# Choosing the early expert with the eight-largest instruction, and loading and converting the second expert's first layer before the first job

## The chip, the cores and the metric

The kernel runs on one core of one Trainium2 chip. The metric is device time in microseconds (us) of one execution; lower is better. Times of before: 698.91 us median of 3 runs (697.92 to 702.77).

## The reference

Three layers follow one another on 3072 tokens of 320 values.

```
attention:  an m-LSTM over 4 x 8 heads of 768 steps, head size 40 (gates f, i, o; state C, n, m)
x = attn_out, as 3072 rows of 320
MoE 1:      logits = x @ w_gate; e = argmax(logits)          # one of 8 experts for each token
            gate_w = softmax(logits)[e];  eom = sigmoid(x @ w_output_gate)
            out[e's tokens] = gate_w * eom * (relu(x @ w1[e]) @ w2[e])     # 320 -> 1024 -> 320
MoE 2:      (sigmoid(x @ w_gate) * (x @ w_val)) @ w_out                    # 320 -> 1536 -> 320
```

## The kernel before

**Stages.** Attention runs in 24 chunks of 128 tokens (`step(n)`, with the order of parts in the tables `ORDER` and `LAST`). While a chunk is in work, the tokens of earlier chunks get their logits (`log`, `lg_`), are routed (`route`, a generator of which the parts named `r:2` and `r:3` take two or three pieces) and are scattered by GpSimd (POOL) into `xs_d` in memory, where each expert has its own stretch of rows. Then come the jobs of MoE 1, one for each expert, from that with the most rows down, and then MoE 2 in 8 groups of 384 tokens.

**The early expert.** After 16 chunks (`EARLY`), `first_expert` picks the expert with the most rows so far. Its number, its first row and its end are put into `first_i`; SyncE (SP) loads them into registers (`first_weights`, L924; `first_end`, L259) and starts loading this expert's weights (`load_weights`, at steps 20, 21 and 22). 256 rows of this expert (`HEAD`) are computed in `Head` while the last chunks are still being routed. `sort_experts` ranks the others when routing ends.

**The jobs.** `Job.up(w1, f)` makes eight slices `f` of the hidden layer: 8 matmuls each, then ScalarE (ACT) writes the high half of relu (L362) and VectorE (DVE) the low half (L363). `Job.down(w2, i)` multiplies 128 rows by the second layer, hidden slice after hidden slice (`k` = 0 to 7, three matmuls each, L373). The first job (`jobs[0]`) holds the remaining 256 of the early expert's 512 slots, so its downs come to 48 matmuls.

**The weights.** An expert's weights arrive as fp32 in a staging tile `ws` (pool `stage`, four buffers) and are split into a high and a low fp16 half by ACT (L118) and DVE (L119), in pieces of at most 512 columns. One expert is six units: units 0 to 2 are the first layer `w1`, two pieces each; units 3 to 5 are `w2`. `Feed` holds the units in order: `load` issues loads up to three units ahead, `pull(budget)` puts in as many pieces as a budget allows (it is called in each `up` and `down`), and `drain(upto)` puts in all pieces up to a unit. `load_next` issues the first loads for the second expert in the tail of attention; `there=step.next` tells the feed so.

**Blank rows.** `blanks(k)` writes filler rows behind an expert's last row in `xs_d`, so that its job can read a full slot; the job's transposing read of `xs_d` (L352) and its small read `own` (L353) come behind them. All of these and the loads of weights are issued from SP's one queue, in its order.

**What sets the order.** Each engine runs its instructions in a fixed order made at build time. The builder places an instruction on its engine by when it expects it to be ready, so the order of calls in the code is not always that of the rows; the rows of the section on the change show what came out.

Of the kernel before, what the change touches and what calls it, by code (L numbers as in the profile page):

```python
# [9 lines left out]
F32 = mybir.dt.float32  # L10
F16 = mybir.dt.float16
U32 = mybir.dt.uint32
I32 = mybir.dt.int32
# [8 lines left out]
T = 128  # L22
# [44 lines left out]
def fused(ctx, tc, a, out, dbg=None):  # L67
# [30 lines left out]
    def constants():  # L98
        G.memset(fill, 0.0)
        G.tensor_copy(fill[:, XW - 2:XW - 1].bitcast(U32), tok[:, NTILE:])  # L100
        split(wgl[:, 0], wgl[:, 1], wgl_s, SG)
        G.tensor_copy(rows_e, ebase)
        G.tensor_copy(table[:, 0], num_e)
        G.tensor_copy(table[:, 1], ebase[0:1])
# [128 lines left out]
    first_e = perm.tile([1, E], F32, name="first_e")  # L233
    first_i = perm.tile([1, 3], I32, name="first_i")
    table = perm.tile([1, 3, E], F32, name="table")
    plan = perm.tile([1, 3, E], U32, name="plan")
    rank = perm.tile([1, 2, E], F32, name="rank")

    def by_tokens(key):

        V.tensor_sub(key, rows_e[0:1], ebase[0:1])
        V.scalar_tensor_tensor(key, key, float(E), last_e, ALU.mult, ALU.add)

    def first_expert():
        f2 = small.tile([1, 4], F32, name="f2", bufs=1)
        by = small.tile([1, 3, E], F32, name="planf", bufs=1)
        G.tensor_copy(table[:, 2], rows_e[0:1])
        by_tokens(key)
        V.tensor_reduce(f2[:, 3:4], key, AX.X, ALU.max)
        yield  # L250
        V.tensor_tensor(first_e, key, f2[:, 3:4].to_broadcast([1, E]), ALU.is_equal)
        V.tensor_tensor(by, table, first_e.unsqueeze(1).to_broadcast([1, 3, E]), ALU.mult)
        V.tensor_reduce(f2[:, 0:3], by, AX.X, ALU.add)
        V.tensor_copy(first_i, f2[:, 0:3])
        yield

    def first_end():

        return nc.sync.value_load(first_i[0:1, 2:3], min_val=0, max_val=(E - 1) * PITCH + EARLY * T)  # L259

    key = perm.tile([1, E], F32, name="key")

    def sort_experts():

        top = small.tile([1, E], F32, name="top", bufs=1)
        by_tokens(key)
        V.scalar_tensor_tensor(key, first_e, 2.0**20, key, ALU.mult, ALU.add)
        V.max(top, key)
        V.max_index(plan[:, 0], top, key)
        V.tensor_scalar_mul(plan[:, 1], plan[:, 0], float(PITCH))  # L270
# [129 lines left out]
    with ExitStack() as att:  # L400
# [521 lines left out]
        def first_weights():  # L922

            e, step.row = (nc.sync.value_load(first_i[0:1, i:i + 1], min_val=0, max_val=(E - 1) * m)  # L924
                           for i, m in enumerate((1, PITCH)))
            return of_expert(e)
# [20 lines left out]
        def load_next():  # L947

            w1, _ = of_expert(place(ranks[1])[0])
            for k in range(3):  # L950
                s = stage.tile([128, F1], F32, name="ws", tag="ws")
                if k == 0:
                    G.memset(s[0:1, 0:8], 0.0)
                SP_.dma_start(out=s, in_=w1[:, k])
                step.next.append(s)
# [320 lines left out]
    with ExitStack() as m1:  # L1276
# [20 lines left out]
        for k, (r, s, n) in enumerate(jobs):  # L1297
            ahead += 0.95 * idle[k]
            if k + 1 < E:
                r1 = ranks[k + 1]  # L1300
                weights[r1] = expert_tiles(wfA if (k + 1) % 2 == 0 else wfB)
                feed.add(expert_units(*weights[r1], lambda r=r1: of_expert(place(r)[0]), there=(None,) * 3 if k else step.next))
# [11 lines left out]
        with tc.manual_schedule(engines=manual):  # L1314
# [17 lines left out]
            at_work = {0: job(0)}  # L1332
            blanks(1)
            feed.load()
            for k, (r, s, n) in enumerate(jobs):
# [4 lines left out]
                rate = feed.left(upto[k]) / idle[k]  # L1340
                w1, w2 = weights[r]
                for f in range(K1):
                    if f == K1 // 2 and k + 2 < len(jobs):
                        blanks(k + 2)
                    cur.up(w1, f, lambda: feed.pull(rate * idle_up(n, f), upto[k]))
# [80 lines left out]
def _constants():  # L1426
# [23 lines left out]
    ctab[..., 2 * TMAX + 1] = E - 1 - np.arange(E)  # L1450
# [41 lines left out]
```

## Time and profile before

| | |
|---|---|
| median of 3 runs | 698.91 us |
| the profiled execution | 699.65 us |
| its span, from the first to the last instruction | 697.9 us |
| TensorE (PE) busy | 669.2 us (96%) |
| VectorE (DVE) busy | 395.0 us (57%) |
| ScalarE (ACT) busy | 301.7 us (43%) |
| GpSimd (POOL) busy | 121.3 us (17%) |
| mean granted TensorE clock | 0.988 |

The profile is of one execution. Busy times overlap, since the engines run side by side; an engine's idle time costs something only where another that sets the end waits for it. The timeline gives the start of each group of instructions from the span's start, how long it took, and in brackets how long the engine was idle just before it and what released it. The stages that matter here lie at 105 to 117 us (the early expert is chosen) and at 138 to 172 us (end of attention, the first job, start of the second job).

### The profile page before, as it was taken

The numbers are of one execution on the slowest core, as the hardware profiler recorded it, in microseconds if no ns is written. First come the engines' busy times: TensorE is split into PE (matmuls) and PEld (weight loads), VectorE is DVE, ScalarE is ACT, GpSimd is POOL, SyncE is SP. The second block draws the span as 40 slices with busy tenths as digits, with TensorE's granted clock in tenths as the row PEclk, the third lists the DMA queues.
The fourth block names the chain that finished last, engine by engine and source line by source line (L and its number), as shares of the span: only waits on it lengthen the run. The fifth ranks groups of instructions, "written<-read, shape, count | busy, mean of one in ns | idle before, by whom it ended". The sixth has DMA issues, their size and how long they took to land. (4 is left out here: it accounts for less than half of the span.)

```text
span 697.9 us, 16215 instructions
## 1 busy us (share of the span) xinstructions
PE 669.2 (96%) x6464; PEld 451.6 (65%) x6464; DVE 395.0 (57%) x930; ACT 301.7 (43%) x710; POOL 121.3 (17%) x192
## 2 busy tenths in 40 slices
PE   7898998798999999999989999999999999999998
PEld 4787887675666757667545576565665655656655
DVE  6688788767778788997858901322404214033131
ACT  2486776564566564654525511222313223133131
POOL 5335766341112222222100000000000000000000
PEclk9999999999999999999999999999999999999999
DMA  6567886569598998966333022001020010000000
GB/s 194 163 191 214 248 238 223 176 194 288 169 271 245 269 284 253 257 170 138 124 92 92 1 72 54 1 20 44 1 63 0 20 44 1 29 1 11 20 1 28
DMA packets 69727, 85.57 MB, mean 123 GB/s; under 512 B 44329, under 2 KB 51914, under 8 KB 69650
## 3 DMA queue, kind: packets, MB, share of 16 engines
q1 hardware_dynamic: 66160, 75.05, 38.8%
q0 software_dynamic: 2896, 9.22, 3.7%
q8 instruction: 51, 0.84, 0.5%
q10 hardware_dynamic: 594, 0.25, 0.2%
q14 instruction: 26, 0.21, 0.1%
HBM read 57.36 MB, written 18.04 MB: 108 GB/s over the span
## 5 line engine op out<-in xcount | busy, mean ns | idle before, releaser
L132 PE MATMUL pa<-xT,wgv 128*128 128x384 f16 x1348 | 226.4, 328 | 3.7 <-DVEq L1369 3.2
L132 PEld LDWEIGHTS <-wgv 128*128 128x128 f16 x1348 | 130.3, 98 | 96.7 <-issue 13.9
L1251 DVE SCALAR_TENSOR_TENSOR gt<-pa,sg 128x384 f32<-128x384 f32 x96 | 52.9, 557 | 219.2 <-ACT sg L1250 204.0
L1269 PE MATMUL pb<-wo,hh 128*128 128x320 f16 x864 | 118.7, 299 | 0.1
L1250 ACT ACTIVATE sg<-pa 128x384 f32<-128x384 f32 x96 | 45.9, 485 | 142.2 <-PE pa L1239 142.0
L1269 PEld LDWEIGHTS <-hh 128*128 128x128 f16 x864 | 84.0, 98 | 34.8 <-issue 2.6
L373 PE MATMUL pb<-w,hh 128*128 128x320 f16 (+4 forms) x624 | 88.3, 303 | 3.0 <-ACT hh L362 2.7
L132 PEld LDWEIGHTS <-w 128*128 128x128 f16 x704 | 61.4, 98 | 31.8 <-issue 0.6
L132 PE MATMUL pa<-xT,w 128*128 128x384 f16 (+5 forms) x576 | 80.8, 301 | 0.0
L373 PEld LDWEIGHTS <-hh 128*128 128x128 f16 (+4 forms) x624 | 63.4, 102 | 26.6 <-ACT hh L362 3.1
L119 DVE SCALAR_TENSOR_TENSOR w<-ws,w 128x512 f16<-128x512 f32 (+1 forms) x92 | 56.6, 642 | 3.3 <-ACT w L118 3.3
L118 ACT ACTIVATE w<-ws 128x512 f16<-128x512 f32 (+1 forms) x92 | 51.2, 591 | 12.3 <-DMA ws<-in_w 12.3
L1255 ACT ACTIVATE hh<-gt 128x384 f16<-128x384 f32 x96 | 49.9, 520 | 10.8 <-DVE gt L1251 10.6
L1256 DVE TENSOR_TENSOR hh<-gt,hh 128x384 f16<-128x384 f32 x96 | 52.8, 550 | 1.6
L1271 ACT ACTIVATE ob<-pb 128x320 f32<-128x320 f32 x24 | 10.5, 437 | 85.1 <-PE pb L1269 85.1
L384 POOL DMA_INDIRECT y_d<-yr,own x24 | 28.8, 1200 | 77.4 <-DVE w L119 24.6
L363 DVE SCALAR_TENSOR_TENSOR hh<-pa,hh 128x384 f16<-128x384 f32 (+6 forms) x80 | 36.2, 479 | 10.7 <-ACT hh L362 10.2
L690 DVE TENSOR_TENSOR pf<-ps,w 128x512 f32<-128x512 f32 x48 | 31.2, 684 | 17.3 <-ACT w L675 6.5
L362 ACT ACTIVATE hh<-pa 128x384 f16<-128x384 f32 (+6 forms) x80 | 33.2, 431 | 13.8 <-PE pa L132 13.2
L720 PE MATMUL po<-vk,pf 128*64 128x41 f32 x768 | 28.7, 234 | 5.8 <-DVE po L709 3.5
L720 PEld LDWEIGHTS po<-vk,pf 128*64 128x64 f32 x768 | 25.9, 141 | 8.1 <-DVE po L709 4.3
L685 PE MATMUL ps<-qk 64*64 64x128 f32 x768 | 29.0, 287 | 1.8 <-issue 0.9
(188 smaller groups left out, 671.5 us busy)
## 6 DMA issues: line engine op xcount, KB each, us to landing
ws<-in_w SPq DMA_DIRECT2D x24, 512.0 KB
vk<-in_vk SPq DMA_DIRECT2D x24, 484.0 KB
qk<-in_qk SPq DMA_DIRECT2D x48, 160.0 KB
ws<-in_w SPq DMA_DIRECT2D x15, 480.0 KB
ws<-in_wg SPq DMA_DIRECT2D x9, 512.0 KB
ws<-in_wv SPq DMA_DIRECT2D x9, 512.0 KB
ws<-in_wo SPq DMA_DIRECT2D x8, 480.0 KB
out<-ob SPq DMA_DIRECT2D x24, 160.0 KB
```

The source lines that it names most:

```text
L118: A.activation(hi, src, AF.Copy, scale=scale)
L119: low = lambda: V.scalar_tensor_tensor(lo, src, scale, hi, ALU.mult, ALU.subtract)
L132: PE.matmul(ps, r if swap else l, l if swap else r, start=fresh and n == 0, stop=whole and n == len(steps) - 1, skip_group_check=not fresh)
L362: A.activation(self.hh[:, 0, f], ph, AF.Relu)
L363: V.scalar_tensor_tensor(self.hh[:, 1, f], ph, 0.0, self.hh[:, 0, f], ALU.max, ALU.subtract)
L373: PE.matmul(py, self.hh[:, x, k, sl], w2[:, y, k, :], start=k == 0 and x + y == 0, stop=k == K1 - 1 and x == 1)
L720: PE.matmul(m.po[sl, h, :], m.pf[g][:, p, sl], m.v41[:, h, :], start=m.first and h == 0, stop=g == 1, skip_group_check=True)
L1250: A.activation(sg, pgv[0], AF.Sigmoid, scale=1.0 / (SY * SWG))
L1251: V.scalar_tensor_tensor(gt, pgv[1], SGT / (SY * SWV), sg, ALU.mult, ALU.mult)
L1255: A.activation(self.gh[:, 0, f, :], box[0], AF.Copy)
L1256: V.tensor_sub(self.gh[:, 1, f, :], box[0], self.gh[:, 0, f, :])
L1269: PE.matmul(po, self.gh[:, x, k, sl], wo[:, y, k * DM:(k + 1) * DM], start=k == 0 and x + y == 0, stop=k == K2 - 1 and x == 1)
```

## The change

The parts:

1. `first_expert` finds the expert by one multiply-add (`by_tokens`; the constant `last_e` in `ctab` now takes the row base off too), `max` and `max_index` (`by_rank`), a multiplication (`starts`) and a copy of the row ends, in three pieces instead of two. The `table` on POOL, its three copies, the comparison, product and sum are gone. `first` holds all eight experts in rank order; `first_end` reads its end at the place given by a register.
2. `load_next` loads two units instead of three; the third comes from the feed.
3. Right after the first job's reads are issued, `feed.load()` and `feed.drain(3)` load units 2 to 5 and convert units 0 to 2, and only then `blanks(1)` follows. The first three slices of the first job pull nothing.

```diff
@@ constants
-        G.tensor_copy(table[:, 0], num_e)
-        G.tensor_copy(table[:, 1], ebase[0:1])
@@
-    def by_tokens(key):
-        V.tensor_sub(key, rows_e[0:1], ebase[0:1])
-        V.scalar_tensor_tensor(key, key, float(E), last_e, ALU.mult, ALU.add)
+    def by_tokens():
+        V.scalar_tensor_tensor(key, rows_e[0:1], float(E), last_e, ALU.mult, ALU.add)
+
+    def by_rank(to):
+        V.max(top, key)
+        V.max_index(to[:, 0], top, key)
+
+    def starts(to):
+        V.tensor_scalar_mul(to[:, 1], to[:, 0], float(PITCH))
 
     def first_expert():
-        f2 = small.tile([1, 4], F32, name="f2", bufs=1)
-        by = small.tile([1, 3, E], F32, name="planf", bufs=1)
-        G.tensor_copy(table[:, 2], rows_e[0:1])
-        by_tokens(key)
-        V.tensor_reduce(f2[:, 3:4], key, AX.X, ALU.max)
+        by_tokens()
         yield
-        V.tensor_tensor(first_e, key, f2[:, 3:4].to_broadcast([1, E]), ALU.is_equal)
-        V.tensor_tensor(by, table, first_e.unsqueeze(1).to_broadcast([1, 3, E]), ALU.mult)
-        V.tensor_reduce(f2[:, 0:3], by, AX.X, ALU.add)
-        V.tensor_copy(first_i, f2[:, 0:3])
+        by_rank(first)
         yield
+        starts(first)
+        V.tensor_copy(first[:, 2], rows_e[0:1])
+        yield
@@ sort_experts
-        by_tokens(key)
+        V.tensor_tensor(first_e, key, top[:, 0:1].to_broadcast([1, E]), ALU.is_equal)
+        by_tokens()
         V.scalar_tensor_tensor(key, first_e, 2.0**20, key, ALU.mult, ALU.add)
-        V.max(top, key)
-        V.max_index(plan[:, 0], top, key)
-        V.tensor_scalar_mul(plan[:, 1], plan[:, 0], float(PITCH))
+        by_rank(plan)
+        starts(plan)
@@ load_next
-            for k in range(3):
+            for k in range(2):
@@ the feed's list of units
-                feed.add(expert_units(..., there=(None,) * 3 if k else step.next))
+                feed.add(expert_units(..., there=(None,) * 3 if k else (*step.next, None)))
@@ ahead of the jobs
             at_work = {0: job(0)}
+            feed.load()
+            feed.drain(3)
             blanks(1)
-            feed.load()
             for k, (r, s, n) in enumerate(jobs):
...
-                rate = feed.left(upto[k]) / idle[k]
+                skip = 0 if k else 3
+                rate = feed.left(upto[k]) / (idle[k] - skip * idle_up(n, 0))
...
-                    cur.up(w1, f, lambda: feed.pull(rate * idle_up(n, f), upto[k]))
+                    cur.up(w1, f, lambda: feed.pull(rate * idle_up(n, f) * (f >= skip), upto[k]))
@@ _constants
-    ctab[..., 2 * TMAX + 1] = E - 1 - np.arange(E)
+    ctab[..., 2 * TMAX + 1] = E - 1 - (E * PITCH + 1) * np.arange(E)
```

Line numbers of the changed kernel are 2 or 3 lower than those of before from here on. In the order of instructions three places move.

On DVE, where the early expert is chosen (behind the reciprocal of a chunk's denominators; `so` and `x` scale the chunk's output, `po` its carried part, `rk` and `m` are routing's), there stands before:

```order
L241 TENSOR_TENSOR key<-rows_e,c_75 1x8
L242 SCALAR_TENSOR_TENSOR key<-key,ctab 1x8
L249 TENSOR_REDUCE f_2447<-key 1x1
L251 TENSOR_TENSOR first_e<-key,f_2447 1x8
L252 TENSOR_TENSOR planf<-table,first_e 1x24
L253 TENSOR_REDUCE f_2447<-planf 1x3
L254 CAST first_i<-f_2447 1x3
L841 TENSOR_TENSOR rk<-rk,oh 128x32
L761 SCALAR_TENSOR_TENSOR so<-so,den 128x320
```

and now:

```order
L236 SCALAR_TENSOR_TENSOR key<-rows_e,ctab 1x8
L239 MAX top<-key 1x8
L240 MAX_INDEX first<-top,key 1x8
L243 TENSOR_SCALAR first<-first 1x8
L251 CAST first<-rows_e 1x8
L758 SCALAR_TENSOR_TENSOR so<-so,den 128x320
```

Seven instructions became five, and routing's `rk` now stands behind `po` instead of ahead of `so`.

On ACT, around the start of the first job (`hh<-pb` are the two evictions of `Head`'s downs, `hh<-pa` the first job's relu slices 0 to 7, `w_3326` the second expert's first layer, `w_3327` its second layer), there stands before:

```order
L118 ACTIVATE w_3326<-ws 128x512 x2
L137 ACTIVATE hh<-pb,hh 128x320 x2
L362 ACTIVATE hh<-pa 128x256
...
L118 ACTIVATE w_3327<-ws 128x512
L362 ACTIVATE hh<-pa 128x256
L118 ACTIVATE w_3327<-ws 128x448
L118 ACTIVATE w_3327<-ws 128x512
L362 ACTIVATE hh<-pa 128x256 x3
```

and now (`w_3316` and `w_3317` in place of `w_3326` and `w_3327`):

```order
L116 ACTIVATE w_3316<-ws 128x512 x3
L135 ACTIVATE hh<-pb,hh 128x320
L116 ACTIVATE w_3316<-ws 128x512 x3
L135 ACTIVATE hh<-pb,hh 128x320
L359 ACTIVATE hh<-pa 128x256 x3
L116 ACTIVATE w_3317<-ws 128x512
L116 ACTIVATE w_3317<-ws 128x448
L359 ACTIVATE hh<-pa 128x256
L116 ACTIVATE w_3317<-ws 128x512
L359 ACTIVATE hh<-pa 128x256
L116 ACTIVATE w_3317<-ws 128x448
L359 ACTIVATE hh<-pa 128x256 x3
```

All six pieces of the first layer now stand ahead of the first relu; the last three relu slices still stand behind unit 4, behind its first piece before and behind both now.

On SP, from the first job's reads on (`hh<-xs_d` is its transposing read and its `own`, `xT<-xs_d` the second job's; a load of 1024 columns is a unit of a first layer, 960, 960 and 640 are units 3, 4 and 5; address instructions left out), there stands before:

```order
L353 DMA hh<-xs_d 128x2x2
...
L108 DMA xs_d<-fill 128x3x322
...
L200 DMA ws<-in_w 128x960
...
L352 DMA_TRANSPOSE xT<-xs_d 128x5x384
...
L353 DMA own<-xs_d 128x3x2
...
L200 DMA ws<-in_w 128x960
...
L200 DMA ws<-in_w 128x640
```

and now:

```order
L350 DMA hh<-xs_d 128x2x2
...
L198 DMA ws<-in_w 128x1024
...
L198 DMA ws<-in_w 128x960
...
L198 DMA ws<-in_w 128x960
...
L198 DMA ws<-in_w 128x640
...
L106 DMA xs_d<-fill 128x3x322
...
L349 DMA_TRANSPOSE xT<-xs_d 128x5x384
```

Units 4 and 5 moved ahead of the second job's blank rows and read; unit 2 moved from the end of `load_next`, ahead of the first job's reads, to behind them.

## Rows read from the trace of the kernel before

**Rows 1.** The page, part 1: busy time, share of the span, instructions.

```profile
PE 669.2 (96%) x6464; PEld 451.6 (65%) x6464; DVE 395.0 (57%) x930; ACT 301.7 (43%) x710; POOL 121.3 (17%) x192
```

**Rows 2.** Waits of PE, whole span: line, releaser, us in total, times, longest.

```profile
PE po L720 <- DVE po L709: 3.5, 4, 2.2
...
PE pb L373 <- ACT hh L362: 2.7, 1, 2.7
```

**Rows 3.** Timeline of PE, first and second job: start, us, instruction, idle before.

```profile
160.50 2.20 PE L373 MATMUL pb<-w,hh 128*128 128x320 f16 x15
165.43 6.29 PE L373 MATMUL pb<-w,hh 128*128 128x320 f16 x33 [2.73 <-ACT hh L362]
171.55 10.56 PE L132 MATMUL pa<-xT,w 128*128 128x384 f16 x64
181.95 9.94 PE L373 MATMUL pb<-w,hh 128*128 128x320 f16 x72
```

**Rows 4.** Timeline of ACT in the first job.

```profile
153.68 0.53 ACT L137 ACTIVATE hh<-pb,hh 128x320 f16<-128x320 f32 x1 [2.94 <-issue]
...
164.47 0.63 ACT L118 ACTIVATE w<-ws 128x512 f16<-128x512 f32 x1 [4.43 <-DMA ws<-in_w]
165.01 0.91 ACT L362 ACTIVATE hh<-pa 128x256 f16<-128x256 f32 x3
```

**Rows 5.** Timeline of SP's queue, 149 to 162 us.

```profile
149.01 1.38 SPq L352 DMA_TRANSPOSE hh<-xs_d  x1
150.62 0.40 SPq L353 DMA_DIRECT2D hh<-xs_d  x1
153.62 0.41 SPq L108 DMA_DIRECT2D xs_d<-fill  x1
...
157.70 1.72 SPq L352 DMA_TRANSPOSE xT<-xs_d  x1
...
160.32 0.93 SPq L200 DMA_DIRECT2D ws<-in_w  x2
```

**Rows 6.** Windows of 2 us: busy us by engine, granted clock, DMA share, GB/s.

```profile
110.00:112.00 2.00, 1.31 (x26) 1.32 (x28) 2.00 (x8) 0.83 (x2) 0.94 (x2) 0.69 0.12 16
112.00:114.00 2.00, 2.00 (x37) 1.81 (x35) 1.69 (x7) 0.16 (x1) 1.16 (x2) 0.50 0.92 285
...
166.00:168.00 2.00, 2.00 (x9) 1.15 (x8) 2.00 (x5) 1.10 (x3) 0.00 (x0) 0.50 0.92 289
...
176.00:178.00 2.00, 2.00 (x14) 1.21 (x13) 2.00 (x5) 1.15 (x3) 0.68 (x1) 1.00 0.00 0
```

**Rows 7.** Timeline of DVE where the early expert is chosen.

```profile
106.61 1.12 DVE L241 TENSOR_TENSOR key<-rows_e,c 1x8 f32<-1x8 f32 x1
107.77 0.39 DVE L242 SCALAR_TENSOR_TENSOR key<-key,ctab 1x8 f32<-1x8 f32 x1
...
109.22 0.47 DVE L761 SCALAR_TENSOR_TENSOR so<-so,den 128x320 f32<-128x320 f32 x1
...
110.13 0.50 DVE L709 TENSOR_TENSOR po<-po,gtm 128x328 f32<-128x328 f32 x1
...
116.92 1.29 DVE L690 TENSOR_TENSOR pf<-ps,w 128x512 f32<-128x512 f32 x2 [1.76 <-PE pu L726]
```

**Rows 8.** Timeline of DVE where the other experts are ranked.

```profile
136.55 0.16 DVE L268 MAX8 top<-key 1x8 f32<-1x8 f32 x1
...
137.00 0.16 DVE L270 TENSOR_SCALAR plan<-plan 1x8 uint32<-1x8 uint32 x1
```

**Rows 9.** Timeline of POOL beside rows 7.

```profile
106.84 0.18 POOL L247 COPY table<-rows_e 1x8 f32<-1x8 f32 x1
107.00 0.71 POOL L695 TENSOR_TENSOR kw<-vk,ktm 128x320 f32<-128x320 f32 x1
```

**Rows 10.** Timeline of PE beside rows 7.

```profile
110.69 1.90 PE L720 MATMUL po<-vk,pf 128*64 128x41 f32 x32 [2.21 <-DVE po L709]
```

**Rows 11.** Waits of PE, 195 to 359 us.

```profile
PE pa L132 <- DMA xT<-y_d: 0.5, 1, 0.5
```

More of the change, by code (lines that the diff above doesn't have):

```diff
@@ L230, in expert_units @@
         return units
[L233 to L236, printed above, removed]
+    first, plan = (perm.tile([1, 3, E], U32, name=n) for n in ("first", "plan"))
     rank = perm.tile([1, 2, E], F32, name="rank")
-    def by_tokens(key):
-        V.tensor_sub(key, rows_e[0:1], ebase[0:1])
-        V.scalar_tensor_tensor(key, key, float(E), last_e, ALU.mult, ALU.add)
@@ L244, in first_expert @@
-    def first_expert():
-        f2 = small.tile([1, 4], F32, name="f2", bufs=1)
-        by = small.tile([1, 3, E], F32, name="planf", bufs=1)
-        G.tensor_copy(table[:, 2], rows_e[0:1])
-        by_tokens(key)
-        V.tensor_reduce(f2[:, 3:4], key, AX.X, ALU.max)
+    key, top = (perm.tile([1, E], F32, name=n) for n in ("key", "top"))
+    def by_tokens():
[3 more added lines that the diff above has]
+        V.max_index(to[:, 0], top, key)
@@ L255, in first_expert @@
         yield
     def first_end():
-        return nc.sync.value_load(first_i[0:1, 2:3], min_val=0, max_val=(E - 1) * PITCH + EARLY * T)
-    key = perm.tile([1, E], F32, name="key")
+        return nc.sync.value_load(first[0:1, 2, bass.ds(step_first[0], 1)], min_val=0, max_val=(E - 1) * PITCH + EARLY * T)
+    step_first = []
     def sort_experts():
-        top = small.tile([1, E], F32, name="top", bufs=1)
-        by_tokens(key)
+        first_e = small.tile([1, E], F32, name="first_e", bufs=1)
+        V.tensor_tensor(first_e, key, top[:, 0:1].to_broadcast([1, E]), ALU.is_equal)
+        by_tokens()
@@ L922, in first_weights @@
         def first_weights():
-            e, step.row = (nc.sync.value_load(first_i[0:1, i:i + 1], min_val=0, max_val=(E - 1) * m)
+            e, step.row = (nc.sync.value_load(first[0:1, i, 0:1], min_val=0, max_val=(E - 1) * m)
                            for i, m in enumerate((1, PITCH)))
+            step_first.append(e)
             return of_expert(e)
@@ L1301, in fused @@
                 weights[r1] = expert_tiles(wfA if (k + 1) % 2 == 0 else wfB)
-                feed.add(expert_units(*weights[r1], lambda r=r1: of_expert(place(r)[0]), there=(None,) * 3 if k else step.next))
+                feed.add(expert_units(*weights[r1], lambda r=r1: of_expert(place(r)[0]), there=(None,) * 3 if k else (*step.next, None)))
                 need.append(len(feed.units))
```

## The prediction

> **What bounds the kernel now.** I read the page's busy times first: TensorE (PE) is busy for 669.2 of the span's 697.9 us [rows 1]. PE sets the end, and only its idle time, or time at a low clock, can be won: 28.7 us of idleness at most. The view of PE's waits comes second, since it names what ends that idleness. Two of its entries lie where the diff works [rows 2]. One wait of 2.2 us is for DVE's `po` (L709), in the chunk in which the early expert is chosen. One of 2.7 us is for ACT's relu `hh` (L362), in the first job.
>
> The second is read in the timelines. PE does 15 of the first job's 48 second-layer matmuls, that is k = 0 to 4 at three each, and stops at 160.50 + 2.20 = 162.70; it goes on at 165.43 [rows 3]. It lacks relu slice 5. ACT wrote slices 5, 6 and 7 at 165.01, because a piece of the second expert's unit 4 stands ahead of them, and ACT sat idle for 4.43 us until that unit's load landed at 164.47 [rows 4]. The load was late because it was issued late: SP's queue had the second job's blank rows (153.62) and its transposing read (157.70) ahead of units 4 and 5 (160.32) [rows 5]. The stall has a second price. The granted clock was 0.50, the lower of TensorE's two levels (1.2 GHz), in the window behind it [rows 6]. The last 33 matmuls took 171.55 - 165.43 = 6.12 us; at the 9.94 / 72 = 0.138 us of the second job's they take 4.56 [rows 3]. The low clock cost 1.56 us.
>
> The first wait has the same shape. DVE begins the chain that picks the expert at 106.61 and starts `so` behind it at 109.22; `po` ends at 110.63 [rows 7], and PE starts at 110.69 after 2.21 us of idleness [rows 10]. In the two windows behind it the granted clock is 0.69 and 0.50, so 0.31 x 2 + 0.50 x 2 = 1.62 us of PE time are lost [rows 6]. That loss is on the path: DVE then waits 1.76 us for PE before 116.92 [rows 7].
>
> **The change: the early expert.** Before, chain and routing's `rk` take 109.22 - 106.61 = 2.61 us. Now five instructions stand there and `rk` comes later. Where the other experts are ranked, `max` and `max_index` together take 137.00 - 136.55 = 0.45 us and the multiplication 0.16 [rows 8]; with 0.16 for the copy, 0.77 us follow the first multiply-add. That one has two bounds. Free, it takes about 0.16 as its neighbours do: the chain is 0.93 us and 1.68 are won. Held up, it ends with GpSimd's `kw`: before, the first `key` instruction took 1.12 us for eight elements [rows 7] and ended at 107.73, when `kw` ended at 107.71 [rows 9]. `kw` now starts earlier by the removed copy, 0.18 us, and ends at 107.53; the chain ends at 107.53 + 0.77 = 108.30, takes 1.69 us, and **0.92 us** are won. I take this value, since the row shows an instruction on the same data being held at this very place.
>
> The Trainium skill bears on this: "SBUF — State Buffer", section "Who interferes with whom", says that a DVE instruction with two SBUF inputs contends with a GpSimd instruction that reads SBUF, and one with a single input does not, outside modes that use both ports. By that rule the new multiply-add, with two inputs, is still held and `max` and `max_index` are not, so the sum would use 0.92; without it, 1.68. The 1.12 us above agrees with the rule, except that the rule gives the lock to whichever starts first, and `key` starts at 106.61, ahead of `kw`.
>
> PE's stall shrinks from 2.21 to 1.29 us (0.53 in the other bound). Does the clock then still fall? The trace has no rule to read off; I take it that it stays up more likely than not, since the idle time nearly halves. That gives **1.62 us**, or nothing.
>
> The rest of this part costs nothing. The ranking of the other experts has six DVE instructions before and after. GpSimd loses three copies. `rk`, `dest` and a reciprocal move back by some places on DVE behind work that PE waits for, which helps it; the scatters that need them come one chunk's work later than the loads of the same step. SP has the expert's number some 0.9 us sooner.
>
> **The change: the first job.** SP's queue after the first job's `own` (150.62 + 0.40) now holds units 2 to 5, then blank rows, then the second job's read. Unit 2 was issued before 149.01, ahead of the first job's reads [rows 5]; it is now issued at about 151.1. Units 4 and 5, issued at 160.32, let ACT go on at 164.47, 4.15 us later, behind a transposing read. So unit 2 is there by 155.2 at the latest. By its bytes alone (512 KB at the 289 GB/s of the window at 166 us [rows 6]) it would be 1.8 us. I take 155.2.
>
> From there ACT's new order runs as follows, with 0.54 us for a piece (164.47 to 165.01), 0.53 for an eviction and 0.91 for three relus [rows 4]. Two pieces of unit 2, to 156.3; eviction, to 156.8; three relus, to 157.7; two pieces of unit 3, to 158.8; relu 3, to 159.1; a piece of unit 4, to 159.65; relu 4, to 159.95; a piece, to 160.5; relus 5 to 7, to 161.4. PE asks for slice 5 at 162.70. ACT is done with that slice at 160.8, 5.6 us after unit 2 has landed, and DVE's half follows, some 0.5 us. So the **2.73 us** of idleness go, and with them the **1.56 us** of low clock: 4.29 us. The work that hides unit 2's lateness is PE's own 64 first-layer matmuls; without this cover each us of lateness past 1.3 us is a us of stall.
>
> What is late next is the second job's read. Units 2 to 5 and the blank rows are 512 + 480 + 480 + 320 + 483 KB = 2.33 MB; at 289 GB/s 8.1 us. If the first starts at 151.1 the blank rows are down by 159.2, and if only when `own` has landed (153.6, when SP went on), by 161.7. The read is issued then, against 157.70 before. It needs between 4.6 us (the first job's, 149.01 to 153.62, smaller) and 6.8 us (157.70 to 164.47, where unit 4 landed behind it): it is there at 163.8 to 168.5. PE wants it at 171.55 - 4.29 = 167.26. Most of this is in time; the worst corner costs 1.2 us. I take nothing for it.
>
> After that the order of work is as before, shifted: the feed's loads are set off by buffers that conversions free, and these stand between PE's slices. The queue has a pause to catch up in: at 176 to 178 us the DMA share is 0.00 [rows 6].
>
> **Sum.** 0.92 + 1.62 + 4.29 = 6.83 us. The profiled execution took 699.65 us, so 692.8. Its own time is 0.7 above the median of the runs shown (698.91); on that footing it is 692.1. I predict 692.8.
>
> **Rivals.**
>
> *The clock falls anyway* at 110 us. For it: 1.29 us of idleness is left, in a stage with small matmuls. Against it: it fell after 2.21. Time: 692.8 + 1.6 = 694.4.
>
> *The early choice is no faster.* The five instructions are held by GpSimd's work one after another, as both `key` instructions seem to have been (1.12 and 0.39 us [rows 7], where 0.16 would do). Then only the first job wins: 699.65 - 4.29 = 695.4. Against it: only one of the new instructions reads two tensors of the kind that was held.
>
> *The win of the first job is eaten.* The second job's read is late, or PE, now ahead, waits on loads later. With 1.2 us it is 694.0; if all of it goes, 699.65 - 2.54 = 697.1. For it: the DMA share is 0.92 at 166 us. Against it: the pause at 176 us, and PE's waits, which from 195 to 359 us come to 0.5 us at the most for one cause [rows 11].
>
> *It gets slower* by unit 2. Its two pieces now stand on ACT ahead of an eviction and of all eight relus. Slice 5 is ready 6.1 us after unit 2 lands, and PE asks for it at 162.7, so a landing later than about 156.5 stalls PE, us for us. At 159.2 the old stall of 2.73 us is back; over 1% slower, 706.0, needs one of 706.0 - 699.65 + 2.54 + 2.73 = 11.6 us, a landing at 168.1, 17 us after issue. The longest load in the rows took 4.15 us, so its chance is small.
>
> **Chances.** Forecast 0.42, clock falls anyway 0.25, early choice no faster 0.08, first job's win eaten in part or whole 0.20, slower 0.05. About 1%, 7.0 us, is what a measurement of this kernel can tell from no change; that border lies at 691.9, just under the forecast. Only a part of the forecast's case lies beyond it, namely with the free multiply-add (0.76 us more) or on the median's footing: 0.22. Slower by over 1%: 0.05. The rest, 0.73, lies within 1%. The range: downwards 692.1 - 0.76 = 691.3, and 0.8 less for the spread of runs (the fastest of before is 1.0 under its median): 690.5. Upwards the eaten win, 697.1, a little rounded: 697.5. Outside it lie slower and a bit of either end.
>
> **What would show it.** In the changed kernel's trace, PE's wait for `hh` in the first job is gone and the granted clock stays 1.00 from 160 to 170 us; the second job's first matmul comes about 6.8 us after the first job's second layer begins (171.55 - 160.50 = 11.05 before [rows 3]). On SP the blank rows come after four loads, near 155 us. DVE takes about 1.7 us from the new multiply-add to `so`, and PE's wait for `po` there is 0.5 to 1.3 us. The prediction is wrong if ACT waits for unit 2 beyond 156.5, if PE waits for the second job's `xT`, if the clock is at 0.50 near 111 us, or if PE shows new waits between 170 and 360 us.

## The result and the profile after

| | before | after |
|---|---|---|
| median | 699.33 us (4 runs, 697.92 to 702.77) | 690.88 us (4 runs, 688.36 to 694.20) |
| profiled execution | 699.65 us | 691.67 us |
| its span | 697.9 us | 689.8 us |
| mean granted clock | 0.988 | 0.990 |

The ratio is 0.988, with a 95% interval of 0.985 to 0.992: 8.4 us by the medians, 8.0 between the two profiled executions. The prediction was 692.8 us, within 690.5 to 697.5, so the time lies at the fast end of the range. It is faster by 1.2%, a case to which the prediction gave 0.22. A run that is over 1.5% longer than the fastest of its kernel is left out of a ratio; that is one run each of `e1` and `e6` below.

The page's busy times and the view of TensorE's (PE's) waits over the whole span (line, releaser, us in total, times, longest), which answer to [rows 1, 2]:

```profile
PE 666.6 (97%) x6464; PEld 450.2 (65%) x6464; DVE 392.9 (57%) x929; ACT 302.1 (44%) x710; POOL 121.4 (18%) x189
```

```profile
PE po L717 <- DVE po L706: 1.5, 3, 0.8
...
PE pa L130 <- DMA hh<-xs_d: 1.0, 1, 1.0
```

The wait for ACT's `hh` is gone from the list, the longest wait for `po` fell from 2.2 to 0.8 us, and a wait for the early expert's transposed rows (`hh<-xs_d`, 1.0 us) is new.

The early choice in the kernel after: the timelines of DVE, GpSimd (POOL) and PE, which answer to [rows 7, 9, 10].

```profile
105.74 0.33 DVE L236 SCALAR_TENSOR_TENSOR key<-rows_e,ctab 1x8 f32<-1x8 f32 x1
106.10 0.16 DVE L239 MAX8 top<-key 1x8 f32<-1x8 f32 x1
...
106.56 0.20 DVE L243 TENSOR_SCALAR first<-first 1x8 uint32<-1x8 uint32 x1
...
106.74 0.47 DVE L758 SCALAR_TENSOR_TENSOR so<-so,den 128x320 f32<-128x320 f32 x1
107.15 0.42 DVE L764 COPY xsb<-tok 128x3 uint32<-128x3 uint32 x1
```

```profile
105.99 0.73 POOL L692 TENSOR_TENSOR kw<-vk,ktm 128x320 f32<-128x320 f32 x1
106.67 0.88 POOL L728 TENSOR_TENSOR Cm<-Cst,Gl 128x164 f32<-128x164 f32 x1
```

```profile
105.90 1.10 PE L682 MATMUL ps<-qk 64*64 64x128 f32 x32
...
108.43 1.13 PE L717 MATMUL po<-vk,pf 128*64 128x41 f32 x32 [0.83 <-DVE po L706]
...
111.11 1.10 PE L682 MATMUL ps<-qk 64*64 64x128 f32 x32
```

From the first instruction of the chain to `so` it is now 106.74 - 105.74 = 1.00 us, where it was 2.61. The new multiply-add takes 0.33 us although `kw` starts while it runs. PE waits 0.83 us in place of 2.21. The 1.38 us won there are 0.23 less than the 1.61 that the chain won: DVE's copy `xsb` behind `so` takes 0.42 us beside GpSimd's `Cm`, where it took 0.15 in the kernel before and takes 0.15 in `e6` and `e8`, with no `Cm` beside it. The 32 `ps` matmuls stand once in every chunk; from those ahead of the wait to those of the next chunk it is 5.21 us, where it was 114.82 - 106.78 = 8.04 in the kernel before. I use this distance below as the length of the stage.

The first job after: timelines of PE, ACT and SP's queue, which answer to [rows 3 to 5].

```profile
150.38 7.15 PE L130 MATMUL pa<-hh,w 128*128 128x256 f16 x64
157.37 6.68 PE L370 MATMUL pb<-w,hh 128*128 128x320 f16 x48
163.89 10.56 PE L130 MATMUL pa<-xT,w 128*128 128x384 f16 x64
```

```profile
151.68 1.15 ACT L116 ACTIVATE w<-ws 128x512 f16<-128x512 f32 x2 [3.07 <-DMA ws<-in_w]
152.73 0.51 ACT L135 ACTIVATE hh<-pb,hh 128x320 f16<-128x320 f32 x1
...
156.93 1.03 ACT L359 ACTIVATE hh<-pa 128x256 f16<-128x256 f32 x3
```

```profile
148.10 2.84 SPq L198 DMA_DIRECT2D ws<-in_w  x4
151.88 0.41 SPq L106 DMA_DIRECT2D xs_d<-fill  x1
158.41 1.95 SPq L349 DMA_TRANSPOSE xT<-xs_d  x1
```

The 48 second-layer matmuls run without a stop. From the first job's first matmul to the second job's it is 163.89 - 150.38 = 13.51 us, where it was 171.55 - 153.52 = 18.03. ACT does wait 3.07 us for unit 2, but its last three relus end at 157.96, and PE reaches those slices later than that.

Windows of 2 us of the kernel after (busy us by engine; the last three figures are granted clock, DMA share and GB/s), which answer to [rows 6]:

```profile
108.00:110.00 2.00, 1.57 (x48) 1.56 (x48) 2.00 (x8) 0.99 (x3) 0.94 (x2) 1.00 0.38 59
110.00:112.00 2.00, 2.00 (x55) 1.73 (x49) 1.92 (x9) 1.47 (x4) 1.40 (x2) 1.00 0.92 332
...
128.00:130.00 2.00, 0.99 (x6) 0.66 (x5) 1.83 (x10) 0.91 (x2) 1.11 (x3) 0.50 1.00 312
...
164.00:166.00 2.00, 2.00 (x14) 1.18 (x12) 1.86 (x6) 0.53 (x1) 1.31 (x2) 1.00 0.87 317
```

The clock is whole behind the early choice and behind the first job. At 126 to 134 us it fell, to 0.76, 0.50, 0.50 and 0.53 in four windows, which is 3.4 us of PE time. The kernel before has a low stretch near there too, half as costly (0.40 x 2 + 0.46 x 2 = 1.7 us):

```profile
124.00:126.00 2.00, 2.00 (x33) 1.64 (x29) 1.35 (x7) 0.75 (x4) 0.00 (x0) 0.60 0.18 55
126.00:128.00 2.00, 2.00 (x35) 1.61 (x33) 1.40 (x6) 1.97 (x6) 0.00 (x0) 0.54 0.17 28
```

**Where the time went.** The span shrank by 8.1 us. The chunk of the choice begins 0.88 us sooner, by work ahead of it that the change leaves alone. The stage of the choice gave 2.83. From there to the first job 0.57 was lost again (39.27 us against 38.70); the low stretch in it cost 1.7 us more than the one of before. The first job gave 4.52, and 0.44 came behind it. The two stages that were changed gave 7.35 us; the prediction had 6.83 for them.

### The profile page after: what moved, and what is told of

The parts are those of the page before. It is cut to its first block, busy times and chain, and to the rows that moved or that the text cites. A ratio compares the mean times of both kernels' runs of the same rounds, so it can differ in the third digit from the quotient of the medians.

```text
span 689.8 us, 16210 instructions
## 1 busy us (share of the span) xinstructions
PE 666.6 (97%) x6464; PEld 450.2 (65%) x6464; DVE 392.9 (57%) x929; ACT 302.1 (44%) x710; POOL 121.4 (18%) x189
## 5 line engine op out<-in xcount | busy, mean ns | idle before, releaser
L370 PE MATMUL pb<-w,hh 128*128 128x320 f16 (+4 forms) x624 | 86.4, 299 | 0.2 <-DVE hh L360 0.2
L381 POOL DMA_INDIRECT y_d<-yr,own x24 | 27.0, 1124 | 73.3 <-DVE w L117 18.0
L672 ACT ACTIVATE w<-pw 128x512 f32<-128x512 f32 x48 | 26.2, 594 | 7.3 <-PE pw L664 6.7
```

What stands on the lines that cost most here:

```text
L370: PE.matmul(py, self.hh[:, x, k, sl], w2[:, y, k, :], start=k == 0 and x + y == 0, stop=k == K1 - 1 and x == 1)
```

## The experiments

Ratios are to the kernel before, run on the same chip in the same series; the medians of before there were 697.86 us (first four) and 697.54 (next four), each from 19 runs or more. The last four (`e8` to `e10` and `r2`) are single runs, beside one of before at 698.22 us, and are read by their profiles alone.

### One half of the change alone

`e1`: the new `first_expert`, `sort_experts` and `constants`, with the first job as before.

```diff
-        by_tokens(key)
-        V.tensor_reduce(f2[:, 3:4], key, AX.X, ALU.max)
+        by_tokens()
         yield
...
+        by_rank(first)
```

> The kernel before with the early choice by the eight-largest instruction alone; loads and conversions of the second expert as before. Theory (two separate stalls, each with its own price): DVE takes about 1.0 us from the new multiply-add to so, as in the changed kernel, PE waits about 0.8 us for po there, and the first job's stall of 2.7 us with its stretch at the lower clock (1.56 us) is still there; the first job, from its first first-layer matmul to the second job's, takes 18.0 us. Time 2.3 to 3.2 us under before, 696 to 697. Rival (the early choice only moves the wait on, to the transposing read of the early expert's rows, on which PE waited 1.0 us in the changed kernel): the first job begins less than 1.5 us earlier than before's 153.5, and the time is within 1 us of before.

Measured: 694.80 us median (10 runs; 694.50 without the one left out), ratio 0.995 (0.991 to 0.998). PE's timeline and one window:

```profile
148.47 7.15 PE L130 MATMUL pa<-hh,w 128*128 128x256 f16 x64 [0.68 <-DMA hh<-xs_d]
...
160.67 6.52 PE L370 MATMUL pb<-w,hh 128*128 128x320 f16 x33 [3.01 <-ACT hh L359]
```

```profile
162.00:164.00 2.00, 2.00 (x10) 1.21 (x9) 1.97 (x7) 0.82 (x3) 0.73 (x1) 0.55 1.00 358
```

The choice behaves as in the whole change (chain 1.00 us, wait 0.82, stage 5.20), and the first job keeps its old stall and the low clock behind it.

`e2`: the first job's part alone, with the old choice.

```diff
-            for k in range(3):
+            for k in range(2):
...
+            feed.drain(3)
+            blanks(1)
```

> The kernel before with the second expert's loads and conversions moved, and the early choice as before. Theory: PE waits 2.2 us for po as before; in the first job no wait for hh and a granted clock of 1.00, and first to second job take 13.5 us in place of 18.0; time 4.3 to 4.9 us under before, about 694.8. Rival (part of the first job's win hangs on the early choice, because the second job's read would be late otherwise): first to second job take over 14.5 us, with a wait for xT, and the time is under 3.5 us better.

Measured: 688.19 us median (4 runs), ratio 0.990 (0.984 to 0.996). That is 9.7 us under before by the medians, about twice what was expected. The first job takes 13.50 us to the second, as expected and as in the whole change. Part of the rest is the clock in other places: summed over windows of 2 us, this execution lost 3.4 us to it over the whole span, that of the kernel before 8.6 and that of the kernel after 7.7. The choice has its old wait. PE's timeline, and the window behind it:

```profile
108.36 1.13 PE L720 MATMUL po<-vk,pf 128*64 128x41 f32 x32 [2.20 <-DVE po L709]
```

```profile
110.00:112.00 2.00, 2.00 (x53) 1.74 (x49) 1.90 (x8) 1.54 (x4) 1.49 (x2) 1.00 0.82 317
```

So the same wait of 2.2 us, which cost 1.45 us of clock in the profile before, cost none here; the stage took 6.58 us. The two halves multiply to 0.9947 x 0.9897 = 0.984, at the lower edge of the interval of the whole (0.985 to 0.992). By the times the whole is not faster than this half alone; that the early choice adds to it is shown by `e1` and by the stage in the profiles.

### What in the first job did it

`e3`: the kernel before with units 3 to 5 issued ahead of the blank rows, and nothing else.

```diff
-            blanks(1)
+            feed.AHEAD = 5
             feed.load()
+            feed.AHEAD = 3
+            blanks(1)
```

> The kernel before with units 3 to 5 issued on SP ahead of the second job's blank rows and read; ACT's order, the conversions' places and the load of unit 2 are those of before. Theory (the stall comes from the place of units 4 and 5 in SP's queue): unit 4 lands before ACT comes to it, the wait of 2.7 us for hh is gone and the clock stays up; since unit 5 must wait for a buffer, blank rows are written 5 to 6 us later than before, the second job's read lands late, and PE waits 0 to 2 us for xT; time 2.5 to 4.3 us under before. Rival (it is the conversions' place between the relus on ACT that makes the stall): ACT still comes late to relu slice 5, PE still waits 2 us or more for hh, and the time is that of before within 1 us.

Measured: 691.86 us median (8 runs), ratio 0.993 (0.989 to 0.996). SP's queue and PE:

```profile
148.49 5.83 SPq L200 DMA_DIRECT2D ws<-in_w  x3
155.29 0.41 SPq L108 DMA_DIRECT2D xs_d<-fill  x1
161.01 1.62 SPq L352 DMA_TRANSPOSE xT<-xs_d  x1
```

```profile
156.84 6.68 PE L373 MATMUL pb<-w,hh 128*128 128x320 f16 x48
165.18 5.04 PE L132 MATMUL pa<-xT,w 128*128 128x384 f16 x30 [1.66 <-DMA xT<-xs_d]
```

The order on SP's queue alone removes the stall of `hh`. It also sends the second job's read out 11.2 us after the first job's start (161.01 - 149.86), and PE waits 1.66 us for it: the first job takes 15.32 us. In the kernel after, the read goes out 8.03 us after the start, and nobody waits. What the conversions put first give is this shorter queue: here the second of the three loads waits 3.5 us on SP for a conversion on DVE to free its buffer, where the four loads of the kernel after wait 0.8 us in all. Unit 2's place behind `own` isn't needed for it, as `e5` shows. The time is 6.0 us under before by the medians, more than the 2.5 to 4.3 that were expected; the stall that went, less the new wait, accounts for 18.03 - 15.32 = 2.71.

`e4`: the kernel after with the blank rows again ahead of the loads.

```diff
+            blanks(1)
             feed.load()
             feed.drain(3)
-            blanks(1)
```

> The changed kernel with the second job's blank rows issued ahead of units 2 to 5 again (its read stays behind them). The blank rows wait for the first job's own to land, some 3 us, and hold the loads behind them on SP. Theory (unit 2's lateness is hidden by only 2 to 3 us): unit 2 lands 3 to 4 us later than in the changed kernel, relu slices 3 to 5 come after PE asks for them, and PE waits 0.5 to 2 us for hh in the first job; time 0.5 to 2 us above the changed kernel, without a stretch at the lower clock. Rival (PE has far more cover): no wait for hh, time within 0.3 us of the changed kernel, or better because the second job's read lands sooner.

Measured: 692.26 us median (10 runs), ratio 0.992 (0.989 to 0.995). ACT and PE:

```profile
161.36 1.15 ACT L116 ACTIVATE w<-ws 128x512 f16<-128x512 f32 x2 [6.21 <-DMA ws<-in_w]
```

```profile
154.42 7.15 PE L130 MATMUL pa<-hh,w 128*128 128x256 f16 x64
163.70 2.18 PE L370 MATMUL pb<-w,hh 128*128 128x320 f16 x14 [2.13 <-DVE hh L360]
166.17 0.58 PE L370 MATMUL pb<-w,hh 128*128 128x320 f16 x3 [0.28 <-DVE hh L360]
167.10 4.38 PE L370 MATMUL pb<-w,hh 128*128 128x320 f16 x31 [0.35 <-DVE hh L360]
171.32 10.56 PE L130 MATMUL pa<-xT,w 128*128 128x384 f16 x64
```

This is the prediction's slower rival, built. Unit 2 is there 6.94 us after the job's start in place of 1.30, and PE stands still for 2.76 us in three pieces, more than the theory's 0.5 to 2. The first job takes 171.32 - 154.42 = 16.90 us, 3.39 more than in the kernel after, with the clock at 1.00. The cover was therefore about 6.94 - 3.39 = 3.6 us after the start; it is some 3.0 in ACT's order of the kernel after, where an eviction of 0.51 us still stands behind unit 2. Of this the kernel after has 1.7 us to spare. The price is read from the profile; the time, 0.992 against 0.988 to 0.990 of the kernel after, can't be told apart.

`e5`: the kernel after with unit 2 loaded where the kernel before loaded it.

```diff
-            for k in range(2):
+            for k in range(3):
...
-                feed.add(expert_units(*weights[r1], lambda r=r1: of_expert(place(r)[0]), there=(None,) * 3 if k else (*step.next, None)))
+                feed.add(expert_units(*weights[r1], lambda r=r1: of_expert(place(r)[0]), there=(None,) * 3 if k else step.next))
```

> The changed kernel, with unit 2 of the second expert loaded where the kernel before loaded it (before the first job's own transposing read) and units 3 to 5 ahead of the blank rows. Theory: ACT's wait of 3.07 us for unit 2 goes, but TensorE had 6 us of second-layer work in hand and did not wait, so the first to second job distance stays at 13.5 us and the time within 1.5 us of the changed kernel's in the same call. Rival 1: the first job's own read of rows, now behind 512 KB more, comes later, and the first job starts up to 1.8 us later (512 KB at the 289 GB/s seen in the kernel before): the time is about 1.8 us longer. Rival 2: the blank rows and the second job's read go out earlier by about 1 us and the time falls by that.

Measured: 688.64 us median (6 runs), ratio 0.988 (0.984 to 0.992); the unaltered kernel after has 690.23 and 0.990 in the same series (`r1`, below), which can't be told apart. ACT's wait is gone and the first job takes 13.50 us all the same. The blank rows and the second job's read go out sooner (5.62 us after the job's start, where `r1` has 8.34), with no gain. The first job starts behind a wait for its own rows, and 1.13 us later than in `r1` when both are counted from the `ps` matmuls ahead of the choice's wait (42.69 us against 41.56), so the first rival holds in part:

```profile
147.97 7.15 PE L130 MATMUL pa<-hh,w 128*128 128x256 f16 x64 [1.32 <-DMA hh<-xs_d]
```

`e7`: the kernel after with the blank rows written twice, so that the second job's read comes later.

```diff
             feed.drain(3)
+            again = blank_rows(end(jobs[1][0]), -(-SLOTS[jobs[1][0]] // T) * T)
...
             blanks(1)
```

> The changed kernel with the second job's blank rows written twice on SyncE's queue, so that its transposing read goes out later by one such write (483 KB, 1.7 us at 289 GB/s, and the wait between the two). What the second write does is repeat the first. Theory: the read had a margin of 1 to 2 us; TensorE then waits 0.5 to 2 us for xT at the start of the second job, and the first to second job distance grows from 13.5 to 14 to 15.5 us. Rival: the margin hides it all, the distance stays at 13.5 us, and the time does not move.

Measured: 691.41 us median (9 runs), ratio 0.991 (0.989 to 0.994). SP's queue and PE:

```profile
151.69 7.19 SPq L106 DMA_DIRECT2D xs_d<-fill  x2
162.25 1.62 SPq L349 DMA_TRANSPOSE xT<-xs_d  x1
```

```profile
166.47 10.56 PE L130 MATMUL pa<-xT,w 128*128 128x384 f16 x64 [2.60 <-DMA xT<-xs_d]
```

The read went out 162.25 - 150.20 = 12.05 us after the job's start, 3.71 later than in `r1`; the first job took 16.27 us, 2.77 more than in `r1`. So the margin in `r1` was 0.9 us: smaller than the theory's 1 to 2, and the delay larger than a write's transfer, since the second write was waited for too. PE began 4.22 us after the issue here and 4.17 in `e3`. By the times (0.991 against 0.990) this run and `r1` can't be told apart.

### What the early choice won, and why

`e6`: the kernel after with eight idle DVE instructions behind `by_rank`.

```diff
+        G.memset(rank, 0.0)
...
         by_rank(first)
+        for _ in range(8):
+            V.tensor_scalar_mul(spare, rank[:, 0], 1.0)
...
+    spare = perm.tile([1, E], F32, name="spare")
```

The `memset` stands where the constants are made and only gives the eight instructions something to read.

> The changed kernel with eight small VectorE instructions, which compute nothing that is used, behind the new chain and ahead of the one-hot row, so that TensorE's wait for po grows from 0.83 us to about 0.83 + 8 x 0.17 = 2.2 us, as in the kernel before. Theory: the time is 1.4 us longer than the changed kernel's in the same call if the clock stays up, and about 3 us longer if a low-clock stretch follows the stall, as it did in two of the three earlier profiles with a stall of 2.2 us. Rival: TensorE's next wait, 1.0 us for the early expert's transposed rows, takes up what is lost ahead of it, and the time is longer by at most 0.4 us.

Measured: 692.91 us median (11 runs; 691.50 without the one left out), ratio 0.991 (0.988 to 0.994), against 690.23 and 0.990 of `r1`: the intervals overlap. PE and the window behind the wait:

```profile
108.93 1.72 PE L721 MATMUL po<-vk,pf 128*64 128x41 f32 x32 [2.25 <-DVE po L710]
```

```profile
110.00:112.00 2.00, 2.00 (x38) 1.82 (x36) 1.82 (x9) 0.16 (x1) 0.96 (x2) 0.50 0.92 367
```

The wait and the fallen clock came back with the delay, and the stage took 8.10 us, 2.90 more than in `r1`. But the first job began only 1.43 us later when both are counted from the `ps` matmuls ahead of the wait (42.99 us against 41.56): half of the loss was taken up in later waits, 1.0 us of it in PE's waits for GpSimd's `kw`, which come to 0.5 us over the span here and to 1.5 in `r1`. The profiled execution was just 0.4 us longer (689.13 against 688.76). Theory and rival each hold a part.

`r1`: the kernel after once more, unaltered.

> The changed kernel once more, unaltered, as the yardstick of this call. Theory: the chain from the key to the one-hot row takes 1.0 us again, TensorE's wait for po is 0.8 us and the first to second job distance 13.5 us, since these follow from the order of the instructions; the low-clock stretch at 126 to 134 us, which cost 3.4 us in the first profile, need not come again, and the profiled time may then be lower by as much. Rival: the stretch belongs to the new code (it follows from the early expert's rows coming late) and is there again, at the same place.

Measured: 690.23 us median (6 runs), ratio 0.990 (0.986 to 0.994). The chain takes 1.01 us, PE's wait is 0.82, the stage 5.20 and the first job 13.50 us. The low clock at 126 to 134 us is not there: all windows from 100 to 180 us stand at 1.00, and the first job starts at 147.47, where it started at 150.38.

```profile
128.00:130.00 2.00, 1.61 (x24) 1.24 (x22) 1.83 (x12) 1.39 (x5) 0.77 (x1) 1.00 1.01 387
```

So the stretch doesn't follow from the code alone. One that cost 3.4 us came in the profiles of after, `e4`, `e7`, `e8` and `e9`, between 126 and 140 us; one that cost 1.7 us came in those of the kernel before (124 to 128), `r2` (130 to 134) and `e10` (138 to 144). What sets it off stays open, and so does whether the change makes the longer one likelier: no profile with the old choice has it.

`r2`: the kernel before once more, unaltered.

> The kernel before once more, unaltered. Theory: the chain takes 2.6 us, TensorE's wait for po 2.2 us, the first to second job distance is 18.0 us with the wait for hh of 2.7 us, since all of it follows from the order of the instructions. What is open is the clock behind the wait for po: it fell in three of the four earlier profiles with a wait of 2.2 us. Theory that the fall depends on more than this wait: it can stay at 1.00 here. Rival: it falls in the kernel before each time, with 1.5 to 2 us lost between 108 and 114 us.

Measured: 697.94 us (one run). The chain takes 2.61 us and PE waits 2.20; the clock falls behind it, with a stage of 8.62 us. In the first job the stall is there, and the low clock behind it is not:

```profile
160.25 2.20 PE L373 MATMUL pb<-w,hh 128*128 128x320 f16 x15
165.53 4.84 PE L373 MATMUL pb<-w,hh 128*128 128x320 f16 x33 [3.07 <-ACT hh L362]
170.21 3.09 PE L132 MATMUL pa<-xT,w 128*128 128x384 f16 x18
```

The 33 matmuls take 4.7 us, not 6.1, and the job 170.21 - 153.27 = 16.94 us, not 18.03.

Three single runs on why the new multiply-add is not held up. `e8` is the kernel after with GpSimd's copy put back ahead of the chain, `e9` with the old subtraction put back instead, `e10` with both (its edit below); no result of what was put back is used.

```diff
     def first_expert():
+        G.tensor_copy(spare2, rows_e[0:1])
+        V.tensor_sub(spare, rows_e[0:1], ebase[0:1])
         by_tokens()
...
+    spare, spare2 = (perm.tile([1, E], F32, name=n) for n in ("spare", "spare2"))
```

> The changed kernel with GpSimd's small copy of the row counts put back ahead of the new chain, as the kernel before had it; the copy is not used. Theory: it is this copy, which starts at the same moment as the first key instruction, that lets GpSimd's work run ahead of VectorE's: key takes about 1.1 us again (it ends when kw ends), the chain 1.7 to 1.8 us in place of 1.00, and TensorE's wait for po 1.5 us. Rival: key stays at 0.3 us and Cm is the one that takes 0.88 us, since what held key in the kernel before was the subtraction's own form.

Measured: 692.10 us, chain 1.78 us, PE's wait 1.37. DVE and GpSimd:

```profile
105.98 1.13 DVE L236 SCALAR_TENSOR_TENSOR key<-rows_e,ctab 1x8 f32<-1x8 f32 x1
```

```profile
106.22 0.18 POOL L246 COPY spare<-rows_e 1x8 f32<-1x8 f32 x1
106.37 0.71 POOL L694 TENSOR_TENSOR kw<-vk,ktm 128x320 f32<-128x320 f32 x1
```

With the copy, `key` ends at 107.11, when `kw` ends (107.08). The theory holds.

> The changed kernel with the old chain's subtraction (row counts less their bases) put back as VectorE's first instruction; its result is not used. GpSimd's copy stays away. Theory (GpSimd's copy is the cause): the subtraction takes 0.15 to 0.35 us and the chain grows by about 0.2 us, to 1.2. Rival (the subtraction's form is the cause): the subtraction takes about 1.1 us, ending with kw, and the chain grows to 1.9 to 2.2 us.

Measured: 693.14 us, chain 1.65 us, PE's wait 1.25. DVE and GpSimd:

```profile
106.74 0.33 DVE L246 TENSOR_TENSOR spare<-rows_e,c 1x8 f32<-1x8 f32 x1
107.00 0.76 DVE L236 SCALAR_TENSOR_TENSOR key<-rows_e,ctab 1x8 f32<-1x8 f32 x1
```

```profile
106.99 0.73 POOL L694 TENSOR_TENSOR kw<-vk,ktm 128x320 f32<-128x320 f32 x1
```

The subtraction is not slow by itself, so the rival falls. But the theory's 1.2 us was too short: the multiply-add now comes second and is held until `kw` ends (107.76 against 107.72).

> The changed kernel with both put back, GpSimd's copy and VectorE's subtraction, neither used: the start of the old chain. Both theories expect the subtraction at 1.1 us and the second key instruction at 0.4, as in the kernel before; TensorE's wait for po then comes to 0.83 + 0.8 to 1.2 us. If it stays at 0.15 to 0.35 us, neither is the cause.

Measured: 694.81 us; the subtraction takes 1.11 us, the multiply-add 0.49, the chain 2.18, and PE waits 1.78, as both theories had it.

One table of the profiles, since the clock varies between executions: PE's wait for `po`, whether the clock fell within the 6 us behind it, the length of the stage, and the first job up to the second.

| profile | wait | clock fell | stage | first job |
|---|---|---|---|---|
| before | 2.21 | yes | 8.04 | 18.03 |
| `r2`, before again | 2.20 | yes | 8.62 | 16.94 |
| `e3` | 2.19 | yes | 8.60 | 15.32 |
| `e6` | 2.25 | yes | 8.10 | 13.51 |
| `e2` | 2.20 | no | 6.58 | 13.50 |
| `e10` | 1.78 | yes | 7.60 | 13.51 |
| `e8` | 1.37 | no | 5.75 | 13.50 |
| `e9` | 1.25 | no | 5.63 | 13.51 |
| `e1` | 0.82 | no | 5.20 | 18.55 |
| `e4` | 0.82 | no | 5.20 | 16.90 |
| `e7` | 0.82 | no | 5.20 | 16.27 |
| after, `r1`, `e5` | 0.82 or 0.83 | no | 5.20 or 5.21 | 13.50 or 13.51 |

With a wait of 1.78 us or more the clock fell in five profiles of six; with 1.37 or less in none of eight.

## Why the prediction was right, and where it was off

**The forecast came true**, with both stages as its two parts and the clock back in each; one term of it was wrong, and part of the rest was luck. Step by step:

*The new multiply-add is held until `kw` ends: wrong.* The prediction had two bounds for the chain, 0.93 and 1.69 us, and took the second, because the old first instruction was held at this place [rows 7]. Measured: 1.00 us. The term was 0.92 us and should have been 1.61. (In the free bound the multiply-add had 0.16 us and took 0.33; what follows it had 0.77 and took 0.64.) The step that failed is the one on GpSimd's copy, which the prediction counted only as 0.18 us by which `kw` starts sooner. `e8` shows that the copy is what put `key` behind `kw`, and `e9` that even without it only the first two-input instruction goes ahead of `kw`. The gain needs both: the copy gone, and one such instruction in place of two.

The Trainium skill's "SBUF — State Buffer", section "Who interferes with whom", lets the order of issue decide which of two contending instructions waits. By the recorded starts two traces agree with it: in the kernel after `key` starts 0.25 us ahead of `kw` and takes 0.33; in `e9` the subtraction goes ahead and `key`, which starts 0.01 us behind `kw`, takes 0.76. Two rows do not agree: in `e8` `key` starts 0.24 us ahead of the copy and is still held; and in the kernel after GpSimd's `Cm` starts 0.07 us ahead of `so` and is the one that takes longer (0.88 us, where it takes 0.46 in `e8`). Why the copy gets in front stays open. Of the two sums that the prediction set beside each other, the one without the hold (1.68) was the nearer.

*PE's wait becomes 1.29 us, or 0.53:* 0.83, between them, for the 1.00 us chain and the work behind it, in which DVE's copy `xsb` gave 0.27 us back. PE won 1.38 us there.

*The clock then stays up, worth 1.62 us: right,* and the table bears it out: at waits of this size it never fell. Together the stage gave 2.83 us where the prediction had 0.92 + 1.62 = 2.54, so the clock's part was 2.83 - 1.38 = 1.45. But only the 1.38 us are in every execution; the rest is won only against an execution in which the old kernel's clock fell, three of the four profiles with the old choice (not `e2`). And a loss in this stage is in part taken up later, half of it in `e6`.

*The first job, 2.73 + 1.56 = 4.29 us: right,* 4.52 between the profiles. The wait is gone, the clock is 1.00, and the second job follows 163.89 - 157.37 = 6.52 us after the second layer begins (predicted 6.8). ACT's last relus end 7.58 us after the job's start (predicted 161.4 - 153.52 = 7.88). Of the two terms the first is the firm one: in `r2` the same stall came without the low clock, and against `r2` the gain is 16.94 - 13.51 = 3.43.

*Unit 2 lands in time: right.* It landed 3.58 us after its issue (151.68 - 148.10; at most 4.15 predicted). `e4` shows the rival's mechanism and its price: with the blank rows first the landing is 5.64 us later against the job's start, and the job takes 3.39 us more. The prediction let a landing up to 156.5 - 153.52 = 2.98 us after the start pass; `e4` bears that out, with a limit of about 3.0 in this order.

*The second job's read is in time: right, by little.* It was issued 8.03 us after the job's start (predicted 5.7 to 8.2). At the 4.2 us that `e3` and `e7` show it landed near 162.6, and PE wanted it at 163.89. The margin is 0.9 to 1.3 us; beyond it, `e3` and `e7` pay for the lateness.

*The rest costs nothing:* borne out by the sum. The new wait for the early expert's rows (1.0 us) is not in `r1`, and `e2` has it with the old choice (1.3 us), so it isn't a cost of the change.

*The sum and the chances.* 6.83 us was short by 0.5 in the changed stages; 0.75 more came from other places that the change leaves alone, and they differ from one execution to the next by more than that. That the time passed the border of 1% is what the prediction tied to the free multiply-add; 0.46 us of it came that way (1.38 won in place of 0.92), and the 0.75 is luck. `e1` and `e2` put the larger half in the first job (ratio 0.990 against 0.995), as the sum did; for how much either half is worth, the intervals are too wide.

`e5` and `e2` have the lowest medians, 688.64 and 688.19 us, but neither can be told from the kernel after (690.23 in the series of `e5`). No version here beats it measurably, and by time alone `e2`, without the early choice, does as well.

## What to carry to other kernels

Look in a queue of transfers for entries that wait for an earlier landing: here a write and a read of that kind stood ahead of loads that wait for nothing, and moving the loads ahead, with the conversions that free their buffers, was worth 3.4 to 4.5 us without a byte less to move. When a load is put later, state the moment at which it starts to cost, and what comes after it in the queue; here the two margins were about 1.7 and 1 us. Take a low-clock stretch that follows a stall as won only with a chance, since the same stall came with it and without it.

## What the runs showed of the hardware

- An eight-element DVE instruction with two inputs took 0.33 us or 1.13, by whether a 0.18 us copy started on GpSimd 0.24 us behind it; with the copy it lasted through the next GpSimd instruction too (to 107.11 us in `e8`, where that one ended at 107.08).
- DVE's work can hold GpSimd as well: `Cm` took 0.88 us beside `so` and 0.46 without it. DVE's small copy beside the same `Cm` took 0.42 us, and 0.15 without it.
- `max` and its index on eight elements took 0.16 + 0.08 + 0.15 us (the index shows as two instructions), and DVE's starts there lie 0.07 to 0.19 us apart, so that five instructions fit between 106.10 and `so` at 106.74.
- Stretches of the lower clock (0.50) move between executions of the same code: at 126 to 134 us in one profile of the kernel after, nowhere from 100 to 180 us in the other. That alone is 3.4 us, beside a change of 8.0.
- Summed over windows of 2 us, each low stretch in the 14 profiles cost 1.70 to 1.72 us of PE's full speed or a multiple of it (3.4, once 8.5), but for those in the last 20 us of a span. A difference of that size between two single executions need not come from a change.
